# One flag per launch in place of one per group of three tiles, in a three-stage attention and mixing kernel

## The chip, the cores and the metric

The kernel runs on one core of a Trainium2 chip. The metric is the device time of one launch in microseconds (us). Changes are judged against the median of repeated runs of the kernel before; the trace comes from one execution that was profiled.

## The reference

Three stages follow one another on a batch of 4, 8 heads, 576 tokens and 64 values per head:

```python
scores = scale * np.matmul(q, k.transpose(0, 1, 3, 2))
kth = np.partition(scores, -32, axis=-1)[..., -32:-31]       # the 32nd largest of 576 in each row
scores = np.where(scores >= kth, scores, -1000000000.0)
attn = softmax(scores); x = attn @ v                           # heads side by side: 4 x 576 x 512
...
gate = sigmoid(causal 5-tap convolution of x over tokens)      # conv_w
x = (gate * (x @ w_val)) @ w_out
...
theta = x @ w_theta
y = w_tok_r @ (x * cos(theta)) + w_tok_i @ (x * sin(theta))    # over tokens
u = x + y; out = u + maximum(u @ w_ch, 0)
```

## The kernel before

The 32 heads are worked in pairs (u = 0 to 15). Each pair's score rows are cut into 9 tiles of 128 rows by 576 columns, so that there are N = 144 tiles; three tiles that follow one another make a group (G = 3, 48 groups). The main loop runs one step per tile, and in each step every stage is called for another tile, as the list STEP orders them. TensorE is PE in all views, VectorE DVE, ScalarE ACT, GpSimd POOL, SyncE SP.

What happens to tile i: `scores_pe` makes the scores in PSUM at step i - 3, `scores_out` copies them to SBUF on ACT (L498). `pick` on DVE takes the 8 largest of each of 6 slices (L521) and draws the 24 largest out of these 48 (L525, L527). `count` on ACT compares the whole row with the 24th and sums the signs (L533); `below` on POOL multiplies scores by signs (L541, tile y, one buffer), and `rest` on DVE takes the 8 largest of y (L546), the next 8 candidates. Once a group is through this, `select` picks the 32nd largest by the count (L556 to L561, the threshold `thr`). `expo` on ACT makes the exponentials with the negated maximum as bias, `mask` on DVE multiplies them by (score >= thr) and sums the row (L611). Then come `turn` (transposes on PE, L624), `close` (the product with v, L704, and the division), the convolution gate, and jobs for the second and third stages (`front`, `back`), whose matrix products are dealt out over the steps as filler for PE, and finish after the loop.

This selection can fail for a row, when the 24th of the candidates or the threshold isn't positive. So `select` has POOL write two bits per row and tile into `bad` (L554 from the 24th largest, L562 from `thr`), PE sums them over the rows with a vector of ones (L571, appended to the step's score bank), ACT adds the six sums up into one word (L576), and at the group's step 7 (LAG = G + FLAG = 7) DVE loads this word into a register (`values_load`, L584) and branches (L587): if it isn't zero, the group's three tiles are done again by maxima one by one (`repair`, L592 to L596). `mask` of a group's first tile stands behind that branch. The tile of scores has LAG + TO + AHEAD = 11 buffers.

The orders of DVE and ACT are those in which the code is written; those of PE, POOL and SP are set by a scheduler that takes dependences and priorities into account.

Of the kernel before, what the change touches and what calls it, by code (L numbers as in the profile page):

```python
# [26 lines left out]
MORE = 3  # L27
STEP = ("count", "expo", "select", "repair", "mask", "close", "mid", "chains", "convert", "pick", "below", "scores_out",
        "turn_out", "rest", "later", "turn", "work_1", "scores_pe", "work_2", "end", "chains", "loads")
TABLED = True  # L30
# [10 lines left out]
CT = (1,)  # L41
FLAG = 4
AHEAD = 3
# [33 lines left out]
@with_exitstack  # L77
def attention_gate_phase_mixer(ctx, tc, qT, kT, vt, w_val, conv_t, w_out, w_theta, w_tok, w_ch, out):
    nc = tc.nc
    P = 128  # L80
    B, S, DM = vt.shape
# [5 lines left out]
    G = 3  # L87
    NSUB = 6
# [72 lines left out]

    said = cp.tile([1, 2 * G], F32, name="said")
# [4 lines left out]
    jobs, later, mid, extras, chains, flowing, fill, apart, at_end = [], [], [], [], [], [], [], [], []  # L167

# [11 lines left out]
    def run(fs):  # L180
        for f in fs:
            f()
# [320 lines left out]
    def group(i):  # L503
        g, k = divmod(i, G)
        if g not in groups:
            d = {}
            for nm, shape in (("cand", [P, G, 8 * NSUB]), ("tops", [P, G, K]), ("acc", [P, G]), ("nmax", [P, G]),
                              ("thr", [P, G]), ("eq", [P, G, K - KC])):
# [39 lines left out]
    def select(g):  # L548


        d = groups[g]
        tops, acc, bad = d["tops"], d["acc"], wk.tile([P, 2, G], F32, tag="bad", name=f"bad_{g}", bufs=2)
        d["bad"] = bad
# [6 lines left out]
        def threshold():  # L560
# [3 lines left out]
        apart.append(threshold)  # L564
        flag(g)

    def flag(g):
        d = groups[g]

        def on_pe(spare):  # L570
            at_end.append(lambda: nc.tensor.matmul(spare[:1, : 2 * G], ones, d["bad"].rearrange("p a g -> p (a g)"),  # L571
                                                   start=True, stop=True))

            def on_act():
                d["flag"] = wk.tile([1, 1], F32, tag="flag", name=f"flag_{g}", bufs=2)
                nc.scalar.activation(said, spare[:1, : 2 * G], AF.Copy, accum_out=d["flag"])  # L576
            return on_act
        extras.insert(0, (2 * G, on_pe))

    def repair(g):  # L580

        d = groups[g]
# [3 lines left out]
        spare = wk.tile([P, S], F32, tag="ct", name=f"spare_{g}")  # L586
        with tc.If(over > 0):  # L587
            for k in range(G):
                src = s_tiles[g * G + k]
                for r in range(K // 8):  # L590
                    top = d["tops"][:, k, 8 * r : 8 * r + 8]
                    nc.vector.max(top, src)  # L592
                    if r < K // 8 - 1:
                        nc.vector.match_replace(spare, top, src, LOWEST)
                        src = spare
                nc.vector.tensor_copy(d["thr"][:, k : k + 1], d["tops"][:, k, K - 1 : K])  # L596

    def expo(i):
        d, k = group(i)
        e = seq[i]  # L600
        e.exp = wk.tile([P, S], F32, tag="e", name=f"e_{i}", bufs=2)
        tabled(e.exp, s_tiles[i], AF.Exp, bias=d["nmax"][:, k : k + 1], scale=1.0)

    def mask(i):
        e = seq[i]
        part = e.part
        if e is part["tiles"][0]:
            part["sums"] = wk.tile([P, 5], F32, tag="sums", name=f"sums_{e.u}_{e.x}", bufs=3)
        d, k = group(i)
        p = s_tiles[i]  # L610
        nc.vector.scalar_tensor_tensor(p, p, d["thr"][:, k : k + 1], e.exp, ALU.is_ge, ALU.mult,  # L611
                                       accum_out=part["sums"][:, e.slot : e.slot + 1])
# [594 lines left out]

    def run_end():
        run(at_end)
        at_end.clear()  # L1210

    def run_mid():
# [9 lines left out]
    def inside(i, f):  # L1222
        if 0 <= i < N:
            f(i)
# [18 lines left out]
    def by_group(i, f):  # L1243
        if i % G == 0:
            inside(i, lambda i: f(i // G))

    def work_1(i):
        t = target(i)
        work(t, t * (1 - FRAC), PARTS[0])

    DO = {
        "count": lambda i: inside(i - 1, count),
        "expo": lambda i: inside(i - LAG + 1, expo),
        "select": lambda i: by_group(i - G - 2, select),
        "repair": lambda i: by_group(i - LAG, repair),
        "mask": lambda i: mask_between(i - LAG),
# [3 lines left out]
        "convert": convert,  # L1260
        "pick": lambda i: i <= N and pick(i),
        "below": lambda i: inside(i - 2, below),
        "scores_out": lambda i: i + AHEAD - 1 in s_psum and scores_out(i + AHEAD - 1),
        "turn_out": lambda i: inside(i - LAG - TO - 1, turn_out),
        "rest": lambda i: inside(i - 3, rest),
        "later": lambda i: run_later(),
# [3 lines left out]
        "work_2": lambda i: work(0.0, 0.0, PARTS[1]),  # L1270
        "end": lambda i: run_end(),
        "loads": lambda i: run(at_step.pop(i, [])),
# [57 lines left out]
```

## Time and profile before

| | |
|---|---|
| median of 3 runs | 936.78 us (930.82, 936.78, 936.98) |
| profiled execution | 933.2 us, its span 931.4 us |
| busy, of the span | PE 84%, DVE 82%, ACT 71%, POOL 49% |
| granted TensorE clock, mean | 0.91 of full speed |

Busy shares are means over stages with different limits. Register loads and branches aren't counted as busy; the profile shows a wait behind them as a wait for DVEq, the sequencer of DVE.

### The profile page before, as it was taken

What the parts mean: (1) busy time and instruction counts of PE and PEld (TensorE: products, weight loads), DVE (VectorE), ACT (ScalarE), POOL (GpSimd) and SP (SyncE); (2) the same over time, 40 slices, a digit from 0 to 9 for tenths busy, and PEclk for the clock granted to TensorE, in tenths of its full rate; (3) what the DMA queues carried; (4) which work ended last, traced back from release to release, by engine and by line L of the source; (5) the groups of instructions that cost most, each with busy time, mean ns of one, the idle gap of its engine ahead of it and who ended that gap; (6) DMA issues with size and microseconds to landing.
All of it is one profiled execution on the core that took longest, in us unless ns stands there. A gap on an engine that the chain in (4) does not pass through costs nothing. (4 is left out here: it accounts for less than half of the span.)

```text
span 931.4 us, 16383 instructions
## 1 busy us (share of the span) xinstructions
PE 786.8 (84%) x4620; PEld 587.1 (63%) x4620; DVE 760.1 (82%) x2944; ACT 661.0 (71%) x1682; POOL 451.7 (49%) x533
## 2 busy tenths in 40 slices
PE   3347686787687897998989889999999999999997
PEld 2224354554355555865777756776868777689897
DVE  2688999897999989998999998989998779444623
ACT  4567677677777689778688789778787897445711
POOL 4455556444455463445366673454678724101620
PEclk9997677877676797998899999999999999999999
DMA  7656545452343322332266565222264420006001
GB/s 195 174 147 171 148 114 145 120 137 73 77 119 86 86 54 63 110 97 54 63 192 172 171 199 143 63 54 63 70 198 136 132 98 2 13 26 207 1 1 52
DMA packets 74695, 98.46 MB, mean 106 GB/s; under 512 B 14304, under 2 KB 35168, under 8 KB 74592
## 3 DMA queue, kind: packets, MB, share of 16 engines
q1 hardware_dynamic: 74592, 97.31, 38.2%
q8 instruction: 37, 0.61, 0.3%
q14 instruction: 66, 0.54, 0.2%
HBM read 50.55 MB, written 13.11 MB: 68 GB/s over the span
## 5 line engine op out<-in xcount | busy, mean ns | idle before, releaser
L541 POOL TENSOR_TENSOR y<-s,n 128x576 f32<-128x576 f32 x144 | 194.9, 1353 | 206.2 <-ACT n L533 94.8
L521 DVE MAX8 cand<-s 128x8 f32<-128x96 f32 x864 | 215.4, 250 | 10.4 <-ACT s L498 10.4
L611 DVE SCALAR_TENSOR_TENSOR s<-s,thr,e 128x576 f32<-128x576 f32 x144 | 149.8, 1040 | 20.3 <-DVEq L587 13.4
L498 ACT ACTIVATE s<-ps 128x256 f32<-128x256 f32 (+1 forms) x288 | 102.8, 403 | 61.6 <-PE ps L571 34.2
L624 PE MATMUL pt<-ident,s 128*128 128x128 f32 x576 | 102.7, 302 | 40.5 <-DVE s L611 22.0
L546 DVE MAX8 tops<-y 128x8 f32<-128x576 f32 x144 | 108.2, 751 | 28.4 <-POOL y L541 28.4
L704 PE MATMUL px<-pT,v 128*64 128x256 f32 (+3 forms) x640 | 117.0, 450 | 11.8 <-ACT pT L643 11.8
L533 ACT ACTIVATE n<-s,tops 128x576 bf16<-128x576 f32 x144 | 111.5, 775 | 12.9 <-POOL y L541 9.2
L624 PEld LDWEIGHTS pt<-ident,s 128*128 128x128 f32 x576 | 71.1, 152 | 72.9 <-issue 34.7
L1045 PE MATMUL py<-w_tok,z 128*128 128x256 f32 (+1 forms) x432 | 114.3, 407 | 0.2
L173 ACT ACTIVATE e<-s,nmax 128x576 f32<-128x576 f32 x144 | 110.4, 767 | 3.0 <-DVE s L611 2.9
L484 PE MATMUL ps<-kh_None,q 128*128 128x256 f32 x240 | 98.0, 416 | 13.9 <-ACT s L498 6.1
L1045 PEld LDWEIGHTS py<-w_tok,z 128*128 128x128 f32 x432 | 77.8, 190 | 18.3 <-PE px L455 0.6
L643 ACT COPY pT<-pt 128x512 f32<-128x512 f32 x128 | 73.0, 570 | 18.8 <-PE px L704 11.9
L525 DVE MAX8 tops<-cand 128x8 f32<-128x48 f32 x432 | 85.2, 197 | 0.1
L704 PEld LDWEIGHTS px<-pT,v 128*64 128x64 f32 (+1 forms) x640 | 46.4, 145 | 60.6 <-issue 25.8
L485 PE MATMUL ps<-kl_None,q 128*128 128x256 f32 x240 | 74.5, 313 | 0.0
L484 PEld LDWEIGHTS ps<-kh_None,q 128*128 128x128 f32 x240 | 49.1, 205 | 34.7 <-ACT s L498 10.8
L484 PE MATMUL ps<-kh,q 128*128 128x256 f32 (+1 forms) x72 | 36.8, 515 | 36.6 <-ACT s L498 20.5
L527 DVE MATCH_REPLACE8 cand<-tops,cand 128x48 f32<-128x48 f32 x288 | 56.8, 197 | 0.0
L485 PEld LDWEIGHTS ps<-kl_None,q 128*128 128x128 f32 x240 | 49.9, 208 | 3.5 <-issue 1.5
L484 PEld LDWEIGHTS ps<-kh,q 128*128 128x128 f32 x72 | 19.4, 270 | 48.9 <-ACT s L498 30.7
(205 smaller groups left out, 1833.9 us busy)
## 6 DMA issues: line engine op xcount, KB each, us to landing
kh_None<-kh_None SPq DMA_DIRECT2D x48, 144.0 KB, 2.6
kl_None<-kl_None SPq DMA_DIRECT2D x48, 144.0 KB, 2.7
v<-in_vt_dram SPq DMA_DIRECT2D x20, 256.0 KB, 2.9
out_dram<-x2T SPq DMA_DIRECT2D x16, 256.0 KB, 2.9
w<-ch SPq DMA_DIRECT2D x16, 256.0 KB, 4.3
w<-theta SPq DMA_DIRECT2D x16, 256.0 KB, 4.7
kh<-kh SPq DMA_DIRECT2D x28, 144.0 KB, 2.6
kl<-kl SPq DMA_DIRECT2D x28, 144.0 KB, 2.7
```

Source lines behind the costliest of these rows:

```text
L173: ins = nc.scalar.activation(out, src, func, **more).ins
L484: nc.tensor.matmul(bank[:, :w], q2, kh[:, lo:hi], start=(j == js[0]), stop=False)
L485: nc.tensor.matmul(bank[:, :w], q2, kl[:, lo:hi], start=False, stop=(j == js[-1]))
L498: nc.scalar.activation(st[:, lo:hi], bank[:, : hi - lo], AF.Copy, scale=0.125)
L521: nc.vector.max(d["cand"][:, k, 8 * x : 8 * x + 8], s_tiles[i][:, x * SUB : (x + 1) * SUB])
L533: nc.scalar.activation(n, s_tiles[i], AF.Sign, bias=d["tops"][:, k, KC - 1 : KC], scale=-(1.0 + 2.0 ** -22), accum_out=d["acc"][:, k : k + 1])
L541: nc.gpsimd.tensor_tensor(y, s_tiles[i], d.pop(("n", k)), ALU.mult)
L546: nc.vector.max(d["tops"][:, k, KC:K], d.pop(("y", k)))
L611: nc.vector.scalar_tensor_tensor(p, p, d["thr"][:, k : k + 1], e.exp, ALU.is_ge, ALU.mult, accum_out=part["sums"][:, e.slot : e.slot + 1])
L624: nc.tensor.transpose(e.pt[:, c, :], p[:, c * P : (c + 1) * P], ident)
L704: nc.tensor.matmul(px[64 * j : 64 * j + 64, :], v[r, c, 64 * j : 64 * j + 64], pT[r, k, :], start=(c == 0), stop=(c == NF), skip_group_che ...
L1045: nc.tensor.matmul(ps, z[:, m * P : (m + 1) * P], W["tok"][:, w, lo:hi], start=(i + k == 0), stop=(i == NF))
```

## The change

The whole kernel becomes a function `mixer` that is built twice into the program. The first pass has no repair: it keeps all thresholds in one tile `thrs` and, for all tiles, the negated largest and the negated 24th largest in one tile `least`, which POOL writes with one instruction per group (`nmax`). After the last group four DVE instructions count the rows that failed, PE and ACT make one word of it, and after the pass every engine loads this word and branches: if it isn't zero, the second pass (`safe`, maxima one by one for all tiles) does everything again. FLAG goes from 4 to 3, so that `expo`, `mask`, `turn` and `close` of a tile come one step earlier, and the tile of scores has 10 buffers.

```diff
-FLAG = 4
+FLAG = 3
...
-STEP = ['close', 'rest', 'below', 'pick', 'select', 'repair', 'mask', 'expo', 'mid', 'chains', 'end', 'turn_out', 'convert', 'turn', 'scores_out', 'later', 'count', 'work_1', 'scores_pe', 'work_2', 'end', 'loads', 'chains']
+STEP = ['close', 'rest', 'below', 'pick', 'nmax', 'select', 'mask', 'check', 'expo', 'mid', 'chains', 'turn_out', 'convert', 'turn', 'scores_out', 'later', 'count', 'work_1', 'scores_pe', 'work_2', 'loads', 'chains']
...
+    keep = ctx.enter_context(tc.tile_pool(name="keep", bufs=1))
+    flag = keep.tile([1, 1], F32, name="flag")
+    mixer(tc, *tensors, flag)
+
+    over = nc.values_load(flag.bitcast(I32), min_val=0, max_val=0x7F000000,
+                          skip_runtime_bounds_check_because="a count of rows")
+    with tc.If(over > 0):
+        mixer(tc, *tensors, None)
...
+    def nmax(g):
+
+        d = groups[g]
+        nc.gpsimd.tensor_scalar(least[:, g * G : g * G + G, :], d["tops"][:, :, 0 : KC : KC - 1], -1.0, None, ALU.mult)
+
     def select(g):
...
-        nc.gpsimd.tensor_scalar(bad[:, 0, :], tops[:, :, KC - 1], 2.0 ** -100, None, ALU.is_le)
-        nc.gpsimd.tensor_scalar(d["nmax"], tops[:, :, 0], -1.0, None, ALU.mult)
...
-            nc.vector.tensor_reduce(d["thr"], d["eq"], mybir.AxisListType.X, ALU.add)
-            nc.gpsimd.tensor_scalar(bad[:, 1, :], d["thr"], 2.0 ** -100, None, ALU.is_le)
...
+        apart.append(lambda: nc.vector.tensor_reduce(thrs[:, g * G : g * G + G], d["eq"], mybir.AxisListType.X, ALU.add))
...
+    def check():
+
+        bad = cp.tile([P, 2], F32, name="bad")
+        worse = wk.tile([P, S], F32, tag="ct", name="worse")[:, :N]
+        nc.vector.tensor_scalar(worse, thrs, 2.0 ** -100, None, ALU.is_le)
+        nc.vector.tensor_reduce(bad[:, 0:1], worse, mybir.AxisListType.X, ALU.add)
+        nc.vector.tensor_scalar(worse, least[:, :, 1], -2.0 ** -100, None, ALU.is_ge)
+        nc.vector.tensor_reduce(bad[:, 1:2], worse, mybir.AxisListType.X, ALU.add)
 
         def on_pe(spare):
-            at_end.append(lambda: nc.tensor.matmul(spare[:1, : 2 * G], ones, d["bad"].rearrange("p a g -> p (a g)"),
-                                                   start=True, stop=True))
...
+            nc.tensor.matmul(spare[:1, :2], ones, bad, start=True, stop=True)
+            return lambda: nc.scalar.activation(said, spare[:1, :2], AF.Copy, accum_out=flag)
+        extras.append((2, on_pe))
...
-    def repair(g):
...
-        over = nc.values_load(d["flag"].bitcast(I32), engines=[EngineType.DVE], min_val=0, max_val=0x7F000000,
-                              skip_runtime_bounds_check_because="a count of rows")
...
-        "repair": lambda i: by_group(i - LAG, repair),
...
+        "nmax": lambda i: None if safe else by_group(i - G - 1, nmax),
+        "check": lambda i: None if safe or i != N + G else check(),
```

DVE before, at the mask of tile 63, the first of group 21, with the end of `pick` of tile 70 ahead of it; of the repair's 24 instructions three are shown:

```order
L521 MAX cand_23_5033<-s_70_5004 128x8
L584 TENSOR_LOAD flag_21_5065
L587 COMPARE_AND_BRANCH
L592 MAX tops_21_4610<-s_63_4501 128x8
L594 MATCH_REPLACE spare_21_5128<-tops_21_4610,s_63_4501 128x576
...
L596 COPY thr_21_4613<-tops_21_4610 128x1
L587 UNCONDITIONAL_BRANCH
L587 UNCONDITIONAL_BRANCH
L611 SCALAR_TENSOR_TENSOR s_63_4501,sums_7_0_5154<-s_63_4501,thr_21_4613,e_63_5051 128x576
```

DVE now, at the same mask (lines have moved: `rest` is L562, `pick` L537 to L543, `mask` L620):

```order
L562 MAX tops_22_4104<-y_66_4224 128x8
L537 MAX cand_23_4292<-s_69_4198 128x8
...
L541 MAX tops_22_4104<-cand_22_4103 128x8
L537 MAX cand_23_4292<-s_69_4198 128x8
L620 SCALAR_TENSOR_TENSOR s_63_3835,sums_7_0_4307<-s_63_3835,thrs_115,e_63_4241 128x576
L665 RECIPROCAL rs_6_1_4312<-rs_6_1_4312 128x5
L562 MAX tops_22_4104<-y_67_4290 128x8
```

The load and the branch are gone, and the mask of tile 63 follows the pick of tile 69 and no longer that of tile 70.

POOL before, from y of tile 67 to y of tile 71:

```order
L541 TENSOR_TENSOR y_67_5031<-s_67_4783,n_67_5012 128x576
L555 TENSOR_SCALAR nmax_22_4818<-tops_22_4816 128x3
L554 TENSOR_SCALAR bad_22_5202<-tops_22_4816 128x3
L655 TENSOR_SCALAR rs_6_1_5159<-sums_6_1_4626 128x5
L541 TENSOR_TENSOR y_68_5112<-s_68_4844,n_68_5072 128x576
L587 UNCONDITIONAL_BRANCH
L541 TENSOR_TENSOR y_69_5189<-s_69_4944,n_69_5174 128x576
L562 TENSOR_SCALAR bad_22_5202<-thr_22_4819 128x3
L555 TENSOR_SCALAR nmax_23_5036<-tops_23_5034 128x3
L554 TENSOR_SCALAR bad_23_5406<-tops_23_5034 128x3
L541 TENSOR_TENSOR y_70_5256<-s_70_5004,n_70_5226 128x576
L541 TENSOR_TENSOR y_71_5308<-s_71_5061,n_71_5293 128x576
```

POOL now, in the same place:

```order
L557 TENSOR_TENSOR y_67_4290<-s_67_4069,n_67_4260 128x576
L567 TENSOR_SCALAR least_116<-tops_22_4104 128x6
L557 TENSOR_TENSOR y_68_4352<-s_68_4132,n_68_4327 128x576
L557 TENSOR_TENSOR y_69_4412<-s_69_4198,n_69_4383 128x576
L567 TENSOR_SCALAR least_116<-tops_23_4293 128x6
L557 TENSOR_TENSOR y_70_4455<-s_70_4251,n_70_4444 128x576
L557 TENSOR_TENSOR y_71_4512<-s_71_4323,n_71_4486 128x576
```

Three small instructions per group have become one, which needs the 24th largest of the group's last tile. In some groups (23 here, tiles 69 to 71) it stands ahead of y of the group's second tile, in others (22, tiles 66 to 68) ahead of y of the third. Counted over all 48 groups, the last of the instructions that read `tops` stood ahead of the second tile's y in 19 groups before and stands there in 20 now; among the first 16 groups these are 8 and 13.

SP now, at the end of the first pass, where before the five stores were its last instructions but for a branch:

```order
L1098 DMA out_0_dram<-x2T_3_10013 512x1x128
L1098 DMA out_0_dram<-x2T_3_10013 256x1x128
L84 TENSOR_LOAD flag_58
L86 COMPARE_AND_BRANCH
L259 DMA rawk_0_10818<-in_kT_dram 64x576
```

What stands behind the branch belongs to the second pass. The other four engines end their first pass with the same two instructions.

## Rows read from the trace of the kernel before

**Rows 1.** Five stretches: length, busy PE, PEld, DVE, ACT, POOL, granted clock, DMA.
```profile
0.00:47.00 47.00, 15.43 (x46) 10.45 (x46) 22.68 (x121) 22.25 (x55) 22.25 (x50) 1.00 0.70 183
47.00:326.00 279.00, 203.85 (x890) 128.35 (x891) 258.77 (x997) 199.86 (x544) 144.37 (x180) 0.76 0.45 119
326.00:605.00 279.00, 254.28 (x1583) 189.97 (x1582) 256.09 (x1024) 227.08 (x572) 149.99 (x163) 0.96 0.41 115
605.00:776.00 171.00, 163.92 (x1088) 128.98 (x1089) 149.19 (x628) 143.90 (x364) 97.30 (x108) 1.00 0.37 102
776.00:931.40 155.40, 149.35 (x1017) 129.35 (x1017) 73.40 (x179) 67.92 (x149) 37.84 (x34) 0.99 0.15 45
```

**Rows 2.** Line 587, the branch: duration (min/median/max ns), then who waited for it.
```profile
L587 DVEq COMPARE_BRANCH  x48: 56/62/72, 43.7 to 805.7; - x48
...
  DVE s L611: 13.4, 24
  DVE tmp L276: 9.0, 17
```

**Rows 3.** Line 584, the load of the flag into a register.
```profile
L584 DVEq TENSOR_LOAD <-flag x48: 303/306/919, 43.1 to 805.3; - x48
```

**Rows 4.** Timeline of DVE: start, us, what, idle before it.
```profile
403.81 0.25 DVE L521 MAX8 cand<-s 128x8 f32<-128x96 f32 x1
403.97 0.81 DVE L611 SCALAR_TENSOR_TENSOR s<-s,thr,e 128x576 f32<-128x576 f32 x1
...
408.56 0.27 DVE L521 MAX8 cand<-s 128x8 f32<-128x96 f32 x1
409.18 0.82 DVE L611 SCALAR_TENSOR_TENSOR s<-s,thr,e 128x576 f32<-128x576 f32 x1 [0.35 <-DVEq L587]
```

**Rows 5.** Waits of DVE from 47 to 326 us: total, times, longest.
```profile
DVE tmp L276 <- DVEq L587: 8.1, 15, 1.7
DVE tops L546 <- POOL y L541: 6.0, 3, 2.3
```

**Rows 6.** Waits of DVE from 326 to 605 us.
```profile
DVE s L611 <- DVEq L587: 10.0, 16, 1.3
```

**Rows 7.** Waits of DVE from 605 to 776 us.
```profile
DVE s L611 <- DVEq L587: 3.0, 7, 0.6
```

**Rows 8.** Groups by line: busy us, mean ns, then idle before them and its releasers.
```profile
L498 ACT ACTIVATE s<-ps 128x256 f32<-128x256 f32 (+1 forms) x288 | 102.8, 403 | 61.6 <-PE ps L571 34.2 <-PE ps L677 9.5 <-PE ps L485 7.7
...
L554 POOL TENSOR_SCALAR bad<-tops 128x3 f32<-128x3 f32 x48 | 24.4, 508 | 15.3 <-DVE cand L521 5.9 <-DVE tops L525 4.4 <-PE ps L628 2.1
L562 POOL TENSOR_SCALAR bad<-thr 128x3 f32<-128x3 f32 x48 | 17.1, 356 | 37.6 <-DVE thr L561 35.8
...
L571 PE MATMUL ps<-bad,ones 128*1 128x6 f32 x96 | 9.3, 168 | 6.0 <-POOL bad L562 6.0
```

**Rows 9.** Timeline around y of tile 70, POOL and DVE.
```profile
416.21 0.82 POOL L554 TENSOR_SCALAR bad<-tops 128x3 f32<-128x3 f32 x1 [1.05 <-DVE cand L521]
417.11 1.28 POOL L541 TENSOR_TENSOR y<-s,n 128x576 f32<-128x576 f32 x1
418.42 0.76 DVE L546 MAX8 tops<-y 128x8 f32<-128x576 f32 x1 [1.14 <-POOL y L541]
```

**Rows 10.** Chain that ended last: a stretch of PE alone, two of its pieces.
```profile
804.71 0.12 PE ps L571 x2
...
864.04 5.59 PE pth L455 x24
```

**Rows 11.** Timeline of the end, ACT and SP.
```profile
920.93 6.78 SPq L1089 DMA_DIRECT2D out_dram<-x2T  x5
925.18 1.54 ACT L1088 COPY x2T<-po 128x512 f32<-128x512 f32 x3 [3.79 <-PE po L1097]
```

**Rows 12.** DMA issues, KB each, us from issue to landing.
```profile
out_dram<-x2T SPq DMA_DIRECT2D x16, 256.0 KB, 2.9
```

**Rows 13.** Line 592, the first instruction of a repair.
```profile
nothing on L592; most used: ['L455', 'L704', 'L624', 'L1045', 'L521', 'L484', 'L485', 'L527', 'L677', 'L525', 'L1064', 'L533', 'L611', 'L628', 'L498', 'L541', 'L173', 'L571', 'L1097', 'L632', 'L351', 'L546', 'L643', 'L680', 'L948']
```

More of the change, by code (lines that the diff above doesn't have):

```diff
@@ L27 @@
 MORE = 3
-STEP = ("count", "expo", "select", "repair", "mask", "close", "mid", "chains", "convert", "pick", "below", "scores_out",
-        "turn_out", "rest", "later", "turn", "work_1", "scores_pe", "work_2", "end", "chains", "loads")
 TABLED = True
@@ L77, in attention_gate_phase_mixer, with mixer @@
 @with_exitstack
-def attention_gate_phase_mixer(ctx, tc, qT, kT, vt, w_val, conv_t, w_out, w_theta, w_tok, w_ch, out):
+def attention_gate_phase_mixer(ctx, tc, *tensors):
     nc = tc.nc
+    keep = ctx.enter_context(tc.tile_pool(name="keep", bufs=1))
[5 more added lines that the diff above has]
+        mixer(tc, *tensors, None)
+@with_exitstack
+def mixer(ctx, tc, qT, kT, vt, w_val, conv_t, w_out, w_theta, w_tok, w_ch, out, flag):
+    nc = tc.nc
+    safe = flag is None
     P = 128
@@ L160, in attention_gate_phase_mixer @@
     nc.gpsimd.memset(magic, MAGIC)
-    said = cp.tile([1, 2 * G], F32, name="said")
+    said = cp.tile([1, 2], F32, name="said")
+    thrs = cp.tile([P, N], F32, name="thrs")
+    least = cp.tile([P, N, 2], F32, name="least")
     taken, lacking = set(), {}
@@ L166, in attention_gate_phase_mixer @@
     owed = [0.0]
-    jobs, later, mid, extras, chains, flowing, fill, apart, at_end = [], [], [], [], [], [], [], [], []
+    jobs, later, mid, extras, chains, flowing, fill, apart = [], [], [], [], [], [], [], []
     last = {}
@@ L506, in group @@
             d = {}
-            for nm, shape in (("cand", [P, G, 8 * NSUB]), ("tops", [P, G, K]), ("acc", [P, G]), ("nmax", [P, G]),
-                              ("thr", [P, G]), ("eq", [P, G, K - KC])):
+            for nm, shape in (("cand", [P, G, 8 * NSUB]), ("tops", [P, G, K]), ("acc", [P, G]),
+                              ("eq", [P, G, K - KC])):
                 d[nm] = wk.tile(shape, F32, tag=nm, name=f"{nm}_{g}", bufs=2 if nm == "cand" else 3)
@@ L546, in rest @@
         nc.vector.max(d["tops"][:, k, KC:K], d.pop(("y", k)))
+    def nmax(g):
+        d = groups[g]
+        nc.gpsimd.tensor_scalar(least[:, g * G : g * G + G, :], d["tops"][:, :, 0 : KC : KC - 1], -1.0, None, ALU.mult)
     def select(g):
+        if safe:
+            return one_by_one(g)
         d = groups[g]
-        tops, acc, bad = d["tops"], d["acc"], wk.tile([P, 2, G], F32, tag="bad", name=f"bad_{g}", bufs=2)
-        d["bad"] = bad
-        nc.gpsimd.tensor_scalar(bad[:, 0, :], tops[:, :, KC - 1], 2.0 ** -100, None, ALU.is_le)
-        nc.gpsimd.tensor_scalar(d["nmax"], tops[:, :, 0], -1.0, None, ALU.mult)
+        tops, acc = d["tops"], d["acc"]
         apart.append(lambda: nc.vector.tensor_tensor(
@@ L580, in repair @@
-    def repair(g):
-        d = groups[g]
-        over = nc.values_load(d["flag"].bitcast(I32), engines=[EngineType.DVE], min_val=0, max_val=0x7F000000,
-                              skip_runtime_bounds_check_because="a count of rows")
[L586 to L596, printed above, removed]
+        apart.append(lambda: nc.vector.tensor_reduce(thrs[:, g * G : g * G + G], d["eq"], mybir.AxisListType.X, ALU.add))
@@ new lines, in one_by_one @@
+    def one_by_one(g):
+        d = groups[g]
+        spare = wk.tile([P, S], F32, tag="ct", name=f"spare_{g}")
+        for k in range(G):
+            src = s_tiles[g * G + k]
+            for r in range(K // 8):
+                top = d["tops"][:, k, 8 * r : 8 * r + 8]
+                nc.vector.max(top, src)
+                if r < K // 8 - 1:
+                    nc.vector.match_replace(spare, top, src, LOWEST)
+                    src = spare
+            nc.vector.tensor_copy(thrs[:, g * G + k : g * G + k + 1], d["tops"][:, k, K - 1 : K])
+        nmax(g)
@@ L598, in expo @@
     def expo(i):
-        d, k = group(i)
         e = seq[i]
         e.exp = wk.tile([P, S], F32, tag="e", name=f"e_{i}", bufs=2)
-        tabled(e.exp, s_tiles[i], AF.Exp, bias=d["nmax"][:, k : k + 1], scale=1.0)
+        tabled(e.exp, s_tiles[i], AF.Exp, bias=least[:, i, 0:1], scale=1.0)
     def mask(i):
@@ L1206, in mask_between @@
                 inside(i, mask)
-    def run_end():
-        run(at_end)
-        at_end.clear()
     def run_mid():
@@ L1245, in by_group, with group_of @@
             inside(i, lambda i: f(i // G))
+    def group_of(g):
+        group(g * G)
     def work_1(i):
@@ L1251, in attention_gate_phase_mixer @@
     DO = {
-        "count": lambda i: inside(i - 1, count),
+        "count": lambda i: None if safe else inside(i - 1, count),
         "expo": lambda i: inside(i - LAG + 1, expo),
         "select": lambda i: by_group(i - G - 2, select),
-        "repair": lambda i: by_group(i - LAG, repair),
+        "nmax": lambda i: None if safe else by_group(i - G - 1, nmax),
+        "check": lambda i: None if safe or i != N + G else check(),
         "mask": lambda i: mask_between(i - LAG),
@@ L1260, in attention_gate_phase_mixer @@
         "convert": convert,
-        "pick": lambda i: i <= N and pick(i),
-        "below": lambda i: inside(i - 2, below),
+        "pick": lambda i: i <= N and (by_group(i, group_of) if safe else pick(i)),
+        "below": lambda i: None if safe else inside(i - 2, below),
         "scores_out": lambda i: i + AHEAD - 1 in s_psum and scores_out(i + AHEAD - 1),
         "turn_out": lambda i: inside(i - LAG - TO - 1, turn_out),
-        "rest": lambda i: inside(i - 3, rest),
+        "rest": lambda i: None if safe else inside(i - 3, rest),
         "later": lambda i: run_later(),
@@ L1270, in attention_gate_phase_mixer @@
         "work_2": lambda i: work(0.0, 0.0, PARTS[1]),
-        "end": lambda i: run_end(),
         "loads": lambda i: run(at_step.pop(i, [])),
```

12 lines of the change are left out of this document (1 added, 11 removed).

## The prediction

> **What bounds the kernel now.** I first cut the span into stretches [rows 1]. The reader is to compare PE and DVE with the length of each. From 47 to 326 us DVE is busy 259 of 279 us and PE 204, at a granted clock of 0.76: DVE sets the pace. From 326 to 605 us they stand level, DVE 256 and PE 254 of 279. From 605 to 776 us PE is busy 164 of 171 us and DVE 149: PE sets the pace, with 7 us of idle time left. After 776 us the chain of waits runs over PE alone for a long while [rows 10], and DVE is busy half of the time. The first 47 us are start-up, in which DVE is busy 23 us.
>
> Then I looked for time on DVE that isn't counted as busy. The load of the flag takes 0.306 us [rows 3] and the branch 0.062 us [rows 2], 48 times each, and instructions behind the branch were held by it 24 and 17 times, for 13.4 and 9.0 us. No repair ran at all [rows 13], so all of this is price without use. By stretch it is 8.1 us of 15 waits [rows 5], 10.0 of 16 [rows 6] and 3.0 of 7 [rows 7]; seven branches have no wait of DVE put down to them, and their gap ended with something else.
>
> **The price of one flag on DVE.** Between a maximum and the mask right behind it there are 403.97 - 403.81 = 0.16 us from start to start; with load and branch between them there are 409.18 - 408.56 = 0.62 us, of which 0.35 are shown as idle [rows 4]. So one flag costs 0.46 us there, 0.11 us more than its visible wait. The mean visible wait is 22.4 / 41 = 0.55 us, which gives 0.66 us. For 48 groups that is 22 us from the one and 32 us from the other. I take waits as they stand in each stretch, plus 0.11 us each.
>
> The Trainium skill ("Advanced Engine Details and Errata", Control Flow Timing) gives a compare-and-branch about 108 ns; by that alone 48 branches would be an estimated 5 us, and the gain would fall to a few us. The trace disagrees: its gap of 0.46 us holds the register load and what follows a taken jump as well, and the measurement decides.
>
> **What of it lies on the path.** From 47 to 326 us: 8.1 + 15 x 0.11 = 9.8 us. DVE with these waits is 258.8 + 8.1 = 266.9 of 279 us, 96%; nothing else is so full. What comes next there is POOL's y, for which DVE already waits 6.0 us [rows 5], so I keep four fifths: 8 us. From 326 to 605 us: 10.0 + 16 x 0.11 = 11.8 us. If all of it went, PE would be at 254 / 267 = 95%, just under the 164 / 171 = 96% that it holds in the next stretch, so it is possible, but the two engines share the pace, and a shorter DVE step uncovers PE: two thirds, 8 us. From 605 to 776 us: 3.0 + 7 x 0.11 = 3.8 us on an engine that has slack; I count a fifth, 0.8 us. One flag lies in the start-up, 0.5 us of which I count nothing. Sum on DVE: 17 us (between 0, if PE or POOL takes over everywhere, and 32).
>
> **PE.** The pair of matmuls on `bad` takes 0.12 us of the chain [rows 10]; where PE sets the pace, behind 605 us, there are 14 flags: 1.7 us, less 0.1 for the one pair that `check` adds. The four DVE instructions of `check` run where DVE is idle half of the time, and PE has other products queued; if that cover failed, PE would stand still for the length of a few short DVE instructions once, under 2 us, since it has to wait for `bad` in its queue. Moving `turn` and `close` a step earlier moves no work onto PE or off it: in PE's order the filler products are at most a few us further ahead at any tile, and the same amount of filler is left when the last scores are made. So the shorter pipeline by itself is worth nothing where PE has no gap [rows 10]: a step's latency at the end is covered by the `back` products of batch 2. In the start-up the first mask comes one step sooner into a DVE with idle time; up to 1 us, counted as 0. The ten buffers of scores go with one step less of life, so they add no wait.
>
> **ACT and POOL.** ACT waited 34.2 us for the flag's matmul in the score bank, behind which its copy of the scores stood [rows 8]; that wait goes, but DVE hardly ever waited for the copy, so the next thing late is DVE itself: nothing. POOL loses 24.4 + 17.1 = 41.5 us of work and a head-of-queue wait of 35.8 us for the threshold [rows 8], and gets 48 instructions twice as wide in place of `nmax`. POOL is half idle; what counts is only whether y comes in time for `rest`. That can go either way (below), between -6.0 us in the first stretch and a loss; I take 0, because the share of groups with the small instruction ahead of the second y is 19 before and 20 now.
>
> **The end.** Each engine now loads the flag and jumps over the second pass. ACT finishes at 926.7 and SP issues its last store at 927.7 us [rows 11]; a store lands 2.9 us after its issue [rows 12]. A load and a branch cost 0.3 to 0.6 us here beside that landing, so the lower bound is 0. For a jump over thousands of instructions there is no row; the nearest are the waits behind the small jumps, up to 1.7 us [rows 5] with a load of up to 0.92 us [rows 3], 2.6 us together. I take 1 us, as the landing covers most.
>
> The Trainium skill ("Runtime: NRT & Kernel Launch", Instruction fetch mechanics) says that a taken branch whose target lies outside the window that has been fetched waits for a DMA to bring it. If one such fetch is estimated like a landing and nothing covers it, the end would be 2.9 us later and not 1; no run here shows it yet.
>
> **Sum.** 17 + 1.6 - 1 = 17.6 us, some 18 us less. Against the profiled execution's 933.2 us that is 915.6 us; against the median of 936.78, which lies 3.6 us above it, 919.2 us. The three runs spread by 6 us. I predict 919 us. A measurement of this kernel tells about 1%, 9.4 us, from no change: below 927.4 us is faster.
>
> **Rivals.**
> (1) *Another engine takes the place.* The DVE time is freed, but PE is the limit from 326 us on (254 of 279 us is nearly as full as DVE), and only the first stretch pays: 8 + 1.6 - 1, less whatever POOL's y takes of it. For it: PE is over 90% in all stretches from 326 us. Against: PE reaches 96% in the third. It gives 6 to 9 us less: 928 to 931. Chance 0.20.
> (2) *More goes with it.* The visible waits are recovered whole (25 us with the 0.11 each), and y comes in time since POOL no longer has 41.5 us of small work and no wait at the head of its queue: of the 6.0 us in the first stretch and similar ones later another 6. It gives 936.8 - 25 - 6 - 1 = 905. Against: so much needs PE at 97% and more over 300 us. Chance 0.11.
> (3) *POOL's queue makes it slower.* Now one instruction must wait for the 24th largest, the end of `pick`, where before the maximum alone set the bias; where it stands ahead of the second tile's y, y starts late and DVE stands at `rest`: 1.14 us at tile 70 [rows 9]. If all 20 such groups paid this and more, since DVE no longer loses 0.46 us in which POOL could catch up, at 1.14 + 0.46 = 1.6 us it would be 32 us against the 18: 936.8 + 14 = 951, slower. It decides from 12 of the 20 on. Against: before, 19 groups had the same order through L554, and in the first stretch only 3 waits on y were seen [rows 5], though 8 of its groups had it so (13 have it now). Chance 0.06.
> (4) *The flag isn't zero*, and everything runs again: over 1,800 us. No repair ran [rows 13], and the new test counts the same two conditions. Chance under 0.01, put to slower.
>
> **How the numbers follow.** Forecast 0.62, the rivals 0.20, 0.11, 0.06 and 0.01. The forecast's own range is 910 to 927, from the two thirds and four fifths going up to nine tenths or down to a half, and 4 us for the runs' spread. The range for 8 in 10 takes in half of rival 1 and rival 2: 904 to 931. Faster by over 1%: nearly all of the forecast (0.60), rival 2 and a tenth of rival 1, 0.73; within 1%: 0.20, most of rival 1 and a little of the others; slower 0.07.
>
> **What the profile after would show.** No L584 or L587 until the last microseconds. The masks would start 0.16 us after the maximum ahead of them, with no wait for DVEq. The stretches that DVE bounds would shrink, the first by about 8 us (counted between the same tiles' masks), the second by as much, the third by 1 to 2. POOL's busy time would fall by some 35 us. PE's busy share up to tile 100 would rise by 2 to 3 points. The prediction is wrong if the waits of `rest` for y in the first stretch grow well above 6.0 us [rows 5], if PE's idle time stays while DVE's grows (rival 1), or if the end behind the last store grows by over 3 us.

## The result and the profile after

The changed kernel takes 911.16 us (median of 4 runs, 909.28 to 911.61) where the kernel before, beside it, takes 935.56 us (4 runs, 930.82 to 936.98): 24.4 us less, a ratio of 0.9744 [0.9705, 0.9783]. The forecast was 919 us, 18 us less.

The page of the changed kernel, its span and busy times:

```profile
span 909.5 us, 15852 instructions
PE 762.9 (84%) x4526; PEld 576.4 (63%) x4526; DVE 756.5 (83%) x2948; ACT 655.8 (72%) x1588; POOL 427.8 (47%) x437
```

DVE's busy time hardly changed, so what it lost was not work. PE's fell by 23.9 us, from 786.8 us in 4620 instructions. Not all of this is work: the same 4526 instructions kept PE busy for 773.5 us in another kernel (the last of the experiments), at a granted clock of 0.916 in place of 0.927.

To see where the time went I cut both traces where DVE begins the `pick` of tiles 48, 96 and 143, so that a stretch holds the same tiles in both. The kernel before, columns as in [rows 1]:

```profile
0.00:288.70 288.70, 187.69 (x806) 118.69 (x807) 245.75 (x970) 196.19 (x529) 148.43 (x198) 0.80 0.51 132
288.70:540.60 251.90, 227.32 (x1363) 167.15 (x1362) 234.28 (x938) 198.54 (x515) 136.85 (x162) 0.92 0.38 105
540.60:784.50 243.90, 230.97 (x1489) 177.97 (x1489) 214.80 (x897) 205.14 (x509) 132.79 (x146) 1.00 0.39 109
784.50:931.40 146.90, 140.85 (x967) 123.30 (x965) 65.30 (x143) 61.12 (x132) 33.67 (x29) 0.99 0.15 48
```

The changed kernel, cut at the same tiles:

```profile
0.00:285.20 285.20, 182.50 (x802) 115.05 (x802) 242.36 (x972) 196.35 (x505) 144.00 (x173) 0.83 0.52 136
285.20:526.90 241.70, 217.12 (x1327) 163.39 (x1326) 236.09 (x940) 199.65 (x490) 129.74 (x126) 0.94 0.39 111
526.90:761.10 234.20, 224.31 (x1452) 176.04 (x1452) 212.88 (x894) 198.49 (x465) 120.89 (x113) 1.00 0.39 110
761.10:909.50 148.40, 138.95 (x948) 121.87 (x948) 65.20 (x145) 61.32 (x131) 33.14 (x26) 0.98 0.16 48
```

The second number is the length of a stretch. The first lost 3.5 us, the second 10.2, the third 9.7, and the tail grew by 1.5: 21.9 us in all. Most came from the second and the third, not from the first, where DVE alone set the pace. In the third, PE is busy 95% before (230.97 of 243.9) and 96% after, at the same granted clock, 1.00; it is the fullest engine in both. Its busy time fell by 6.7 us there, with 37 matmuls fewer. The flag's 30 matmuls were 2.9 us of it; the rest lies in other products, since FLAG moves some of them across the cuts (the flag's matmuls before: length, PE, PEld, granted clock, DMA):

```profile
540.60:784.50 243.90, 2.91 (x30) 1.28 (x30) 1.00 0.39 109
```

DVE's timeline in the changed kernel at the mask of tile 64, which answers to [rows 4]:

```profile
398.99 0.24 DVE L537 MAX8 cand<-s 128x8 f32<-128x96 f32 x1
399.15 0.80 DVE L620 SCALAR_TENSOR_TENSOR s<-s,thrs,e 128x576 f32<-128x576 f32 x1
```

From maximum to mask it is 0.16 us again; the 0.62 us with load and branch are gone everywhere.

DVE's waits for y, over the whole span (total us, times, longest): first the kernel before, then the changed one.

```profile
DVE tops L546 <- POOL y L541: 28.4, 16, 5.4
```

```profile
DVE tops L562 <- POOL y L557: 34.1, 19, 5.2
```

They grew by 5.7 us. In the first stretch they went from 6.0 us, 3 times [rows 5], to this (45 to 285 us):

```profile
DVE tops L562 <- POOL y L557: 9.9, 6, 2.2
```

### The profile page after: what moved, and what is told of

The parts are those of the page before. It is cut to its first block, busy times and chain, and to the rows that moved or that the text cites. A ratio compares the mean times of both kernels' runs of the same rounds, so it can differ in the third digit from the quotient of the medians.

```text
span 909.5 us, 15852 instructions
## 1 busy us (share of the span) xinstructions
PE 762.9 (84%) x4526; PEld 576.4 (63%) x4526; DVE 756.5 (83%) x2948; ACT 655.8 (72%) x1588; POOL 427.8 (47%) x437
## 4 chain that ended last, share of the span: by engine, by line
DVE 48%; PE 32%; issue 6%; ACT 6%; DMA 4%; POOL 3%; SPq 1%; POOLq 0%; ACTq 0%; DVEq 0%
DVE cand L537 9%; DVE tops L562 7%; PE py L1054 7%; DVE s L620 5%; PE px L713 5%; DVE tmp L293 4%; PE ph L471 4%; DVE cand L543 4%; DVE gp L768 3%; DVE tops L541 3%; PE py L1073 3%; PE pval L471 3%; PE pt L633 2%; PE px2t L471 2%; PE pth L471 2%
## 5 line engine op out<-in xcount | busy, mean ns | idle before, releaser
L557 POOL TENSOR_TENSOR y<-s,n 128x576 f32<-128x576 f32 x144 | 198.2, 1376 | 224.1 <-ACT n L549 86.3
L537 DVE MAX8 cand<-s 128x8 f32<-128x96 f32 x864 | 210.3, 244 | 10.4 <-ACT s L514 10.4
L620 DVE SCALAR_TENSOR_TENSOR s<-s,thrs,e 128x576 f32<-128x576 f32 x144 | 141.3, 981 | 2.8 <-ACT e L189 2.8
L562 DVE MAX8 tops<-y 128x8 f32<-128x576 f32 x144 | 108.0, 750 | 34.1 <-POOL y L557 34.1
L633 PE MATMUL pt<-ident,s 128*128 128x128 f32 x576 | 100.4, 299 | 40.3 <-DVE s L620 21.1
L713 PE MATMUL px<-pT,v 128*64 128x256 f32 (+3 forms) x640 | 111.9, 447 | 14.4 <-ACT pT L652 12.5
L189 ACT ACTIVATE e<-s,least 128x576 f32<-128x576 f32 x144 | 110.8, 770 | 2.9 <-DVE s L620 2.6
L500 PE MATMUL ps<-kh_None,q 128*128 128x256 f32 x240 | 95.2, 403 | 15.5 <-ACT s L514 10.8
L541 DVE MAX8 tops<-cand 128x8 f32<-128x48 f32 x432 | 82.7, 191 | 0.1
L768 DVE SCALAR_TENSOR_TENSOR gp<-xT,w_conv,gp 128x576 f32<-128x576 f32 (+2 forms) x60 | 53.7, 895 | 2.3 <-POOL gp L760 1.6
L543 DVE MATCH_REPLACE8 cand<-tops,cand 128x48 f32<-128x48 f32 x288 | 55.1, 191 | 0.0
```

Of the source, the lines that this page charges most:

```text
L189: ins = nc.scalar.activation(out, src, func, **more).ins
L500: nc.tensor.matmul(bank[:, :w], q2, kh[:, lo:hi], start=(j == js[0]), stop=False)
L537: nc.vector.max(d["cand"][:, k, 8 * x : 8 * x + 8], s_tiles[i][:, x * SUB : (x + 1) * SUB])
L541: nc.vector.max(top, c)
L557: nc.gpsimd.tensor_tensor(y, s_tiles[i], d.pop(("n", k)), ALU.mult)
L620: nc.vector.scalar_tensor_tensor(p, p, thrs[:, i : i + 1], e.exp, ALU.is_ge, ALU.mult, accum_out=part["sums"][:, e.slot : e.slot + 1])
```

## The experiments

The kernels were measured in three series, and those of one series share their runs of the kernel before. Ratios are to it, with a 95% interval; where two experiments of different series are compared, it is by these ratios.

**What the branch and what the making of the flag are worth** (first series, kernel before 931.45 us). The first kernel is the one before without the call of `repair`:

```diff
-        "repair": lambda i: by_group(i - LAG, repair),
+        "repair": lambda i: None,
```

> The kernel before, without the load of the flag and the branch on DVE (the repair is left out, so a failed row would not be mended); the POOL, PE and ACT instructions that make the flag, and FLAG = 4, stay. Theory D (the price is DVE's load and branch): 16 to 22 us less than before, that is 914 to 920. Theory P (most of it is the flag's matmul on PE in the score bank and what waits for it): at most 10 us less, 926 or more. Theory L (the shorter pipeline): at most 10 us less as well.

Measured: 923.67 us, 0.9896 [0.9861, 0.9931]. With load and branch gone and nothing else, only 1.0% goes. Its trace cut at the same tiles (284.6, 529.1 and 775.1 us) shows where: the first stretch is 4.1 us shorter, the second 7.4, the third 2.1 longer, at a granted clock of 0.99 there in place of 1.00. The waits for y are longer than in either kernel above:

```profile
DVE tops L546 <- POOL y L541: 41.5, 28, 5.2
```

The second kernel also leaves out the making of the flag (the two `bad` on POOL, the pair of matmuls, the sum on ACT):

```diff
-        tops, acc, bad = d["tops"], d["acc"], wk.tile([P, 2, G], F32, tag="bad", name=f"bad_{g}", bufs=2)
-        d["bad"] = bad
-        nc.gpsimd.tensor_scalar(bad[:, 0, :], tops[:, :, KC - 1], 2.0 ** -100, None, ALU.is_le)
+        tops, acc = d["tops"], d["acc"]
...
-            nc.gpsimd.tensor_scalar(bad[:, 1, :], d["thr"], 2.0 ** -100, None, ALU.is_le)
...
-        flag(g)
```

> As the run without the branch, and the flag itself left out too: no instruction on bad on POOL, no matmul on PE, no sum on ACT (failed rows are not found at all). FLAG = 4. Theory D: within 3 us of the run without the branch. Theory P: 6 to 12 us below it, near 911. Theory L: both stay 5 us or more above the changed kernel.

Measured: 912.73 us, 0.9786 [0.9736, 0.9836]. What the forecast held for 1.6 us of PE and nothing else brought 10.9 us beside the kernel without branch. The third stretch of both, the one without branch first:

```profile
529.10:775.10 246.00, 233.76 (x1494) 179.70 (x1492) 218.71 (x898) 204.97 (x509) 135.20 (x147) 0.99 0.39 108
```

```profile
526.10:762.70 236.60, 227.18 (x1454) 177.74 (x1452) 218.34 (x897) 201.83 (x473) 114.90 (x114) 0.99 0.41 113
```

It is 9.4 us shorter, and 6.6 of these are busy time of PE. The granted clock is 0.99 in both.

**What the other parts of the change are worth** (same series). The changed kernel with the old number of steps, and the changed kernel without load, branch and second pass:

```diff
-FLAG = 3
+FLAG = 4
```

> The changed kernel with FLAG = 4, so that the pipeline is as long as before (11 score buffers). Theory D and theory P: within 2 us of the changed kernel, 909 to 913. Theory L: 5 us or more slower than it, 916 or more.

```diff
-    over = nc.values_load(flag.bitcast(I32), min_val=0, max_val=0x7F000000,
...
-    with tc.If(over > 0):
-        mixer(tc, *tensors, None)
```

> The changed kernel without the load, the branch and the second pass behind it (the flag is made and not read). All theories: what the end costs, taken as 1 us in the forecast with bounds 0 and 2.9: 908 to 911. If the far jump waits for a fetch that nothing covers, 908.

Measured: 916.96 us, 0.9832 [0.978, 0.9884], with the longer pipeline; 906.34 us, 0.9724 [0.9674, 0.9774], without the end. Against the changed kernel (0.9744 and, run again, 0.9761) the pipeline step is worth 0.7 to 0.9% and the end 0.2 to 0.4%; the intervals overlap, so only the traces below make more of it.

**Which part of the flag costs** (second series, kernel before 935.01 us). From the kernel without branch: one without the `bad` on POOL, in which the pair sums a constant, and one that keeps `bad` and has no pair and no sum:

```diff
-            at_end.append(lambda: nc.tensor.matmul(spare[:1, : 2 * G], ones, d["bad"].rearrange("p a g -> p (a g)"),
+            at_end.append(lambda: nc.tensor.matmul(spare[:1, : 2 * G], ones, counts.rearrange("p g k -> p (g k)")[:, : 2 * G],
```

> As the run without branch (FLAG = 4, no load, no branch), but PE multiplies a constant tile by the ones and ACT sums that, so their 96 matmuls and 48 sums stay, while nothing of it waits for POOL and POOL's two instructions on bad are gone (no row is tested). Theory W (the price of the chain is waiting: PE and ACT stand in order behind bad, which waits for the threshold on DVE): within 3 us of the run without the chain, 912 to 916. Theory K (the price is the work on PE and ACT, which sets the pace behind tile 96): 919 to 924, near the run without the branch. Theory Q (the price is POOL's queue): 912 to 916 as theory W; the next run tells these two apart.

```diff
         apart.append(threshold)
-        flag(g)
```

> As the run without branch, with POOL's two instructions on bad kept and nobody reading them: no matmul on PE, no sum on ACT (no row is tested). Theory Q (POOL's 41.5 us of work and its wait for the threshold make y late): 919 to 924, near the run without the branch. Theory W and theory K: 912 to 916, near the run without the chain.

Measured: 924.09 us, 0.9876 [0.9835, 0.9917], with the pair and the sum; 917.43 us, 0.9822 [0.9787, 0.9857], with POOL's share alone. Nearly the whole price is the pair's or the sum's: 0.9% above the kernel without any flag (0.9786). That the pair waits for POOL is not the cause, since the constant is always there. POOL's share is 0.4%, inside the intervals: it stays open whether it is worth 2 or 3 us or nothing.

The changed kernel run again, and the kernel without any flag with the shorter pipeline:

> The changed kernel unchanged, beside the other runs of this call. All theories: its ratio to the kernel before is again 0.970 to 0.978.

```diff
-FLAG = 4
+FLAG = 3
```

> The run without the chain with FLAG = 3, that is the shorter pipeline alone on top of it, with nmax on POOL as before and no load, branch or second pass at the end. Theory S (the step is worth 3 us in the tail and 2 us ahead of it, as the two pairs of traces so far have it): 5 us below the run without the chain, 906 to 909. Theory N (no value, as forecast; the difference between those pairs comes from nmax and from where POOL's instructions stand): 911 to 914.

Measured: 910.8 us, 0.9761 [0.9714, 0.9809], and 910.42 us, 0.9747 [0.9713, 0.978]. The second is 0.4% under the kernel without flag that has FLAG 4, between the two theories, and the intervals of the two overlap. The tails of both, from the pick of tile 143 to the end, FLAG 4 first:

```profile
762.70:910.40 147.70, 141.38 (x969) 123.81 (x967) 63.94 (x143) 61.08 (x128) 33.51 (x26) 0.99 0.16 47
```

```profile
763.70:908.10 144.40, 138.39 (x946) 121.81 (x944) 64.55 (x141) 61.13 (x129) 33.09 (x26) 0.99 0.16 48
```

The tail is 3.3 us shorter, and PE has 23 matmuls fewer in it: they now stand ahead of the cut. The whole spans are 2.3 us apart, 910.5 and 908.2.

**Is it the pair, its place, or the sum behind it** (third series, kernel before 931.74 us). One theory was that the pair, which is appended to the score bank at the step's end, holds back ACT's copy of the scores [rows 8], and with it PE. In the kernel with the constant I put the pair right behind the scores, and in another I left out ACT's 48 sums:

```diff
-            at_end.append(lambda: nc.tensor.matmul(spare[:1, : 2 * G], ones, counts.rearrange("p g k -> p (g k)")[:, : 2 * G],
-                                                   start=True, stop=True))
+            nc.tensor.matmul(spare[:1, : 2 * G], ones, counts.rearrange("p g k -> p (g k)")[:, : 2 * G],
+                             start=True, stop=True)
```

> As the run with the flag of a constant, but its pair of matmuls is written directly behind the scores of its bank and no longer at the end of the step, behind the filler products: the same number of instructions on PE and ACT, one matmul in front of it instead of 3 to 16. Theory B (the price is the copy of the scores on ACT, which waits for the last matmul that writes its bank, and so for the filler in front of it): 5 to 8 us below the run with the flag of a constant, that is 0.978 to 0.982 of the kernel before. Theory K (the price is the 96 matmuls and 48 sums themselves): within 2 us of it, 0.985 to 0.990.

```diff
-            def on_act():
-                d["flag"] = wk.tile([1, 1], F32, tag="flag", name=f"flag_{g}", bufs=2)
-                nc.scalar.activation(said, spare[:1, : 2 * G], AF.Copy, accum_out=d["flag"])
-            return on_act
+            return lambda: None
```

> As the run with the flag of a constant, without ACT's 48 sums (the flag stays in PSUM and is not read): the matmuls stand at the end of the step as before. Theory B: within 2 us of the run with the flag of a constant, 0.985 to 0.990. Theory K, if the work is ACT's: 0.978 to 0.982.

Measured: 919.17 us, 0.9878 [0.9841, 0.9914], and 920.43 us, 0.9886 [0.9852, 0.992]. ACT's wait for the pair, first with the pair at the step's end, then with the pair at once:

```profile
ACT s L498 <- PE ps L568: 34.4, 19, 3.5
```

```profile
ACT s L498 <- PE ps L568: 15.1, 11, 2.5
```

More than half of the wait went and the ratio stayed at 0.988, so the theory of the held copy falls. So does the sum. What is left, by exclusion, is the pair on PE.

**Is y's single buffer the next limit?** The changed kernel with two buffers for y:

```diff
-        y = wk.tile([P, S], F32, tag="y", name=f"y_{i}")
+        y = wk.tile([P, S], F32, tag="y", name=f"y_{i}", bufs=2)
```

> The changed kernel with two buffers for y, so that POOL can make the next y before DVE has read the last one. Theory Y (part of what DVE gained is given back at rest, which waits 34 us in total for y in the changed kernel, 20 us of it between 45 and 760 us): 3 to 8 us below the changed kernel, 903 to 908. Theory N (these waits come from y being started by ACT's count and by POOL's other work, not by the buffer): within 2 us of it, 909 to 913.

Measured: 911.2 us, 0.9795 [0.9746, 0.9844], and DVE waits for y as long as with one buffer:

```profile
DVE tops L562 <- POOL y L557: 34.4, 19, 5.6
```

So the buffer isn't what y waits for; what y waits for is ahead of it, in its inputs or in POOL's queue; which, this run doesn't tell.

**What the branch costs where no flag is made** (same series). The changed kernel, in which DVE once per group also loads a word that is always zero and branches on it, in front of the mask as before; nothing is added on PE, ACT or, per group, POOL:

```diff
+    nought = cp.tile([1, 1], F32, name="nought")
+    nc.gpsimd.memset(nought, 0.0)
...
+        over = nc.values_load(nought.bitcast(I32), engines=[EngineType.DVE], min_val=0, max_val=0x7F000000,
...
+        with tc.If(over > 0):
...
+        "probe": lambda i: None if safe else by_group(i - LAG, probe),
```

> The changed kernel with one load of a word that is zero and one branch per group put back on DVE ahead of the first tile's mask; no flag on POOL, PE or ACT. If DVE's load and branch cost what the run without the branch showed: 7 to 10 us above the changed kernel, 0.982 to 0.987 of the kernel before. If they cost what the forecast had for DVE: 17 us, 0.993.

Measured: 930.55 us (10 runs), 0.9981 [0.9964, 0.9998]: 19.4 us more than the kernel with two buffers for y (911.2 us) in the same series, 1.9 to 2.4% by the ratios of that kernel and of the changed kernel, and nearly the time of the kernel before. The branch's line, its duration (min/median/max ns) and who waited for it:

```profile
L603 DVEq COMPARE_BRANCH  x48: 56/56/72, 39.4 to 796.8; - x48
...
  DVE s L639: 13.7, 28
  DVE tmp L294: 8.6, 18
```

The visible waits, 22.3 us, are as long as before, 22.4 us [rows 2]. Its trace cut at the same tiles, up to tile 143:

```profile
0.00:286.80 286.80, 185.20 (x802) 117.24 (x802) 242.27 (x972) 196.97 (x505) 141.75 (x174) 0.82 0.50 135
286.80:537.00 250.20, 219.36 (x1331) 163.34 (x1330) 237.66 (x941) 200.08 (x489) 119.79 (x126) 0.94 0.37 108
537.00:780.50 243.50, 230.50 (x1456) 180.77 (x1453) 216.23 (x895) 200.35 (x468) 112.49 (x113) 0.97 0.37 106
```

Against the changed kernel they are 1.6, 8.5 and 9.3 us longer. In the third the granted clock is 0.97, where the changed kernel had 1.00, and nearly the same matmuls (1456 and 1452) keep PE busy 6.2 us longer. The clock stood at 0.50 in two parts of it:

```profile
543.40:553.60 10.20, 10.20 (x38) 5.89 (x36) 6.29 (x36) 3.65 (x10) 2.67 (x3) 0.50 0.75 230
666.30:669.70 3.40, 3.40 (x16) 3.36 (x16) 3.37 (x7) 3.35 (x9) 1.76 (x1) 0.50 0.55 164
```

That is 1.2 GHz in place of 2.4 for 13.6 us, in which PE was busy throughout; by an estimate half of it, 6.8 us, is lost. The first part begins behind a wait of PE for DVE of 2.7 us.

## Why the forecast held, point by point

**The price on DVE.** The forecast took 17 us of 25, the visible 22.4 with 0.11 us on top of most. Two comparisons measure it, and they differ. Taken out of the kernel before, the branch gives 1.0%, 7.8 us by the medians, which is rival 1's figure of 6 to 9 us; put back into the changed kernel it costs 19.4 us. So 17 is right beside the second and twice too much beside the first.

The traces show where the two part. In the first two stretches the branch is worth 4.1 + 7.4 = 11.5 us in the one comparison and 1.6 + 8.5 = 10.1 in the other. In the third it is -2.1 and 9.3 us, and there the granted clock fell in the trace that looks too slow each time: in the kernel with the branch put back as shown, and in the one without the branch here:

```profile
539.80:546.60 6.80, 5.81 (x15) 3.46 (x15) 6.77 (x35) 1.19 (x3) 3.39 (x6) 0.50 0.73 239
```

Half of these 6.8 us is 3.4, the most that was lost. With the clock's share taken off, the spans give an estimate of 9.4 + 3.4 = 12.8 us for the branch taken out and 18.5 - 6.8 = 11.7 for the branch put back: some 12 us both times, five less than the forecast's 17. So nothing here shows that DVE and PE hide one another; most of the difference between the two lies in TensorE's clock. The same holds for the making of the flag, which seems to be worth next to nothing while the branch stays (0.9981, though with the shorter pipeline and the end): the 6.8 us lie in that comparison too. Whether the branch brings the lower clock is open. For it: all ten runs of the kernel with the branch put back have a mean granted clock of 0.902 to 0.920, the eight of the changed kernel 0.920 to 0.927. Against: the kernel before has the branch and kept 1.00 in its third stretch behind a like wait of PE, 3.1 us, and the kernel with the flag of a constant has no branch and shows 0.97 there.

By stretch the forecast had it in the wrong places: 8, 8 and 0.8 us on DVE. Its cuts lie elsewhere, but the first stretch gave 3.5 us and the third 9.7. Of the 9.8 us that the forecast saw on the path in the first, waits for y took 3.9 (from 6.0 to 9.9 us; longer ones were a sign of being wrong that it had named), and the start-up took 2.1: the pick of tile 24 starts at 140.51 us where it did at 138.46, with 18 masks ahead of it for 17. The changed kernel with FLAG 4 has it at 137.51 us, again behind 17 masks. That would leave 3.8; no run took the two apart. The later y is the mechanism of rival 3, and it came to 5.7 us of longer waits over the whole span, not 32.

**PE: the term that was mis-sized.** The forecast counted 14 pairs at 0.12 us, 1.6 us. It read the duration of the pair from the chain of waits [rows 10] and left out what the pair does to the matmul ahead of it. PE's timeline of before:

```profile
802.93 1.78 PE L1045 MATMUL py<-w_tok,z 128*128 128x320 f32 x6
804.64 0.19 PE L571 MATMUL ps<-bad,ones 128*1 128x6 f32 x2
804.76 0.66 PE L624 MATMUL pt<-ident,s 128*128 128x128 f32 x4
```

and PE's timeline of the changed kernel, where the same matmuls stand ahead of a transpose:

```profile
785.63 1.51 PE L1054 MATMUL py<-w_tok,z 128*128 128x320 f32 x5
786.98 0.60 PE L633 MATMUL pt<-ident,s 128*128 128x128 f32 x4
```

Five of them take 786.98 - 785.63 = 1.35 us to the next start, 0.27 each. Six ahead of the pair take 804.64 - 802.93 = 1.71, where 6 x 0.27 = 1.62 would be expected: 0.09 more. With the 0.12 to the transpose behind it a pair costs 0.21 us, and 48 of them 10 us. The three kernels with the pair and without the branch (0.9876, 0.9878, 0.9886) lie 0.9 to 1.0% above the one without (0.9786), 8 to 9 us. The sizes agree. The same reckoning for 43 pairs of the trace of before gives a median of 0.22 us. What is shown is that the price hangs on the pair and on neither its place nor its wait nor the sum behind it. Where it falls is clear in part. Among the kernels without branch whose clock stayed at 1.00 in the third stretch are the one with the pair at once and the changed one with FLAG 4, which has no pair; the former first:

```profile
528.60:768.40 239.80, 230.78 (x1489) 178.28 (x1488) 219.64 (x898) 203.87 (x505) 115.77 (x114) 1.00 0.40 111
526.60:762.80 236.20, 225.60 (x1454) 176.76 (x1452) 219.33 (x898) 201.38 (x473) 123.94 (x114) 1.00 0.40 113
```

They are 3.6 us apart, and 16 pairs at 0.22 us are 3.5, though the two differ on POOL as well. The 9.4 us between the kernels with and without the flag hold more than that: with POOL's share alone the stretch is 240.5 us long, 3.9 more than without any flag, all three at 0.99. Some 2 us are left over, and the price of the other 32 pairs isn't traced to a stretch.

**ACT.** Nothing was counted for the 34.2 us in which the copy stood behind the pair, and the kernel with the pair at once shows that this was right for the 19.3 us of it that went there.

**The shorter pipeline** was counted as nothing, "as a step's latency at the end is covered". Two comparisons point the same way: 0.4% without the flag, 0.7 to 0.9% in the changed kernel. The traces show 3.3 us less in the tail and 2.3 in the whole span. So it is worth some 2 or 3 us and perhaps up to 8; the intervals leave it open between these.

**The end.** The forecast took 1 us, and named growth by over 3 us behind the last store as a sign of being wrong. From the end of the last store's issue to the end of the span it grew by 2.1 us, from 931.4 - 927.71 = 3.7 to 909.5 - 903.66 = 5.8. From the end of ACT's last copy there were 931.4 - 926.72 = 4.7 us before [rows 11]. The last instructions of ACT and SP in the changed kernel:

```profile
899.87 1.54 ACT L1097 COPY x2T<-po 128x512 f32<-128x512 f32 x3 [3.79 <-PE po L1106]
900.48 3.18 SPq L1098 DMA_DIRECT2D out_dram<-x2T  x3
```

and in the one without load, branch and second pass, whose span is 904.0 us:

```profile
898.27 1.54 ACT L1092 COPY x2T<-po 128x512 f32<-128x512 f32 x3 [3.79 <-PE po L1101]
898.88 1.92 SPq L1093 DMA_DIRECT2D out_dram<-x2T  x3
```

That gives 909.5 - 901.4 = 8.1 us and 904.0 - 899.8 = 4.2: 3.9 us for the end, which the medians' 0.2 to 0.4% (2 to 4 us) bear out. SP is the one that ends it. Its load and its branch, with the first instruction behind the jump:

```profile
L84 SPq TENSOR_LOAD <-flag x1: 1212/1212/1212, 903.7 to 903.7; - x1
```

```profile
L86 DVEq COMPARE_BRANCH  x1: 76/76/76, 899.5 to 899.5; - x1
L86 ACTq COMPARE_BRANCH  x1: 50/50/50, 901.0 to 901.0; - x1
L86 DVEq EVENT_SEMAPHORE  x1: 21/21/21, 902.4 to 902.4; - x1
L86 ACTq EVENT_SEMAPHORE  x1: 17/17/17, 904.4 to 904.4; - x1
L86 SPq COMPARE_BRANCH  x1: 45/45/45, 905.0 to 905.0; - x1
L86 SPq EVENT_SEMAPHORE  x8: 17/17/17, 907.6 to 908.1; - x8
```

The load takes 1.21 us where the flag's took 0.306 [rows 3], and SP stands 2.6 us between the branch at 905.0 and its next instruction at 907.6. The stores' median from issue to landing is 3.2 us, and the last issue ends at 903.66; so they have landed by some 906.9 us, and the jump lasts 0.7 us beyond that, with eight semaphores behind it. The cover that the forecast counted on, the landing, is shorter than load and jump in a row.

The Trainium skill ("Runtime: NRT & Kernel Launch", Instruction fetch mechanics) says that a taken branch out of the fetched window waits for a DMA that brings its target, and the forecast gave 2.9 us for that if nothing covered it. The trace agrees: the queues that carry instructions move 9 packets from 895 us on (packets, MB, share of 16 engines; the last row is the stores'),

```profile
q14 instruction: 7, 0.06, 1.3%
q8 instruction: 2, 0.03, 1.1%
...
out_dram<-x2T SPq DMA_DIRECT2D x4, 256.0 KB, 3.2
```

where the last 14.4 us of the kernel before show one, and the last 14 of the kernel without load, branch and second pass none.

The same skill's figure for a compare-and-branch ("Advanced Engine Details and Errata", Control Flow Timing), 108 ns, an estimated 5 us for 48, isn't borne out as the price of such a test: 8 to 19 us were measured for 48 branches with their loads.

**The signs named in advance.** L584 and L587 are gone, and masks start 0.16 us behind the maximum. POOL lost 23.9 us (451.7 to 427.8), not 35: one `least` takes 0.75 us by the median where `nmax` took 0.24. PE's busy share up to tile 96 didn't rise: (187.69 + 227.32) / 540.6 = 77% before, (182.50 + 217.12) / 526.9 = 76% after, since PE's busy time fell by 15.4 us there, with 40 matmuls fewer and a granted clock of 0.83 and 0.94 for 0.80 and 0.92.

**The sum.** Forecast: 17 + 1.6 - 1 = 17.6 us. One chain of kernels leads from before to after in single steps: the branch out, the making of the flag out, the shorter pipeline, and last the one test with the new instruction on POOL. By the spans of their traces these steps are 9.4, 11.5, 2.3 and -1.3 us (931.4, 922.0, 910.5, 908.2, 909.5), 21.9 in all; by the medians the whole is 24.4. The branch on DVE pays as forecast in kind, but with some 12 us and not 17. The end costs more than the 1 us forecast, the making of the flag brought 8 to 11 us where 1.6 was forecast for PE and nothing for POOL, and the shorter pipeline more than nothing. These errors partly cancel: that the forecast's range holds the result is in part luck.

## What to carry to other kernels

The worth of one edit can read twice as large in one kernel as in another, here 7.8 and 19.4 us for the same branch. Before this is put down to engines that hide one another, cut both traces at the same work and compare the granted clock of each stretch: here an estimated 3.4 and 6.8 us came from TensorE at half its clock. A tiny matmul costs more than its own duration, so read the start of the instruction ahead of it to the start of the one behind it, and compare with the same stretch without it. A test that is moved to the end of a launch is not hidden by the last store if its load and jump come behind that store on the same queue.

## What was not expected of the hardware

A pair of matmuls with one column of weights makes the interval of the 320-column matmul ahead of it 0.36 us in place of 0.27. A jump to a far place took 2.6 us on SP, 2.9 on DVE and 3.4 on ACT, from the branch to the next instruction, where load and jump over a repair's 24 instructions together put 0.46 us between two instructions of DVE [rows 4]. The same register load took 0.3 us in the main loop and 1.2 us on SP while the last stores were landing.
